# A scan and a two-layer network on one core: another plan of issue, other start

## The chip, the cores and the metric

The kernel runs on one core of a Trainium2 chip. Its time is the device time of the core in microseconds. TensorE (PE in the rows) does the matrix products, VectorE (DVE), ScalarE (ACT) and GpSimd (POOL) work on elements, and SyncE (SP) issues nearly all DMA transfers. Each engine takes its own instructions in the order in which they were issued; semaphores connect them.

## What is computed

Four batches of eight heads with 768 steps go through a scan with decay `a`, in chunks; its output, 3072 tokens of 256 values, goes through two matrices with `h - tanh(h)` between. The two matrices come in fp64 and are made into fp32 on the chip. Cut to what matters, with the reference's chunk length:

```python
log_a = np.log(np.clip(a, 1e-06, 1.0))
for c in range(nc):                      # chunks of the sequence
    cum = np.cumsum(la, axis=-1)
    L = np.exp(cum[:, :, :, None] - cum[:, :, None, :]) * causal
    M = np.einsum('bhin,bhjn->bhij', Cc, Bc) * L
    y[:, :, sl] = M @ xc + (Cc @ state) * np.exp(cum)[..., None]
    state = decay_full * state + sum_j(Bc_j x_j * decay_from_j)
h = x @ w_in                             # x: y as 3072 x 256; w_in: 256 x 2048
out = (h - np.tanh(h)) @ w_out           # w_out: 2048 x 256
```

## The kernel before

**Tiles.** The sequence is cut into chunks of 112 steps, and the 16 state rows of a chunk ride along as the first of 128 rows. There are 28 chunks (seven for each batch); the four batches' chunks follow one another, and their tokens make eight tiles, four of 256 and four of 512 tokens. Tiles 0 and 1, and 2 and 3, are worked as wide tiles 8 and 9 after the first sweep. The weights are cut into eight units of 256 columns of w_in and 256 rows of w_out. A sweep takes two units over tiles 0 to 3, so that the later units can be loaded and converted meanwhile; tiles 4 to 7 then run over all units.

**One chunk.** A mask `lt` (the exponential of differences of cumulated logs) is multiplied by the product `att` of B and C, cut to its causal part by GpSimd, and multiplied with x by TensorE into `y`. The product `z`, or eight more products behind `y`, gives the state that four small ScalarE copies put into the `x` of the chunk of the same batch that follows. For the first four chunks the mask comes from `fn_k`, `fn_f` and `fn_x` in `first_tile` (lines 445 to 471): GpSimd lays out the logs as `lm`, TensorE multiplies them by a triangle into the bank `cp`, ScalarE takes exp. Chunks 4 to 9 get it by `chunk_a` from rows in `lt_c` and `rt_c`, later ones by a DMA and eight exps in `chunk_l`.

**Products with the weights.** fp32 values are split into a high part (`xh`, `wh`, `gh`) and a low part (`xl`, `wl`, `gl`), and a product is three products of parts (L767 for `x @ w_in`, called mm1; L848 for w_out, mm2). Units 0 and 1 with tile 0 (L760) and their w_out with tiles 0 to 3 (L838) are done in plain fp32 with unsplit `xf`, `wv` and `wf`. `conv` makes fp32 from the raw fp64 words: a scaled ScalarE copy `wv` (L326), a shift of the low word by 29 bits `wm`, by ScalarE for the units named in `EASED` (L332, an affine copy) and by VectorE for the others (L334), a clamp (L339), two joins of bits (L342, L349), and the split (L353, L356).

**Order.** `Order` collects every step with its engine, a cost in microseconds and the names it reads and writes. `schedule` plays the steps through by these costs, `search` does so 16 times with shaken priorities and keeps the shortest plan, and `issue` emits the steps in order of their planned starts. So costs and rules of the planner set the order on every engine. The hardware's waits come from the data, not from the plan.

Of the kernel before, what the change touches and what calls it, by code (L numbers as in the profile page):

```python
# [61 lines left out]
EASED = 0, 1, 2, 3  # L62


class Order:
# [3 lines left out]
    DMA_LATENCY, SEM, SEM_PE, RATE, FLIGHT = 0.8, 0.15, 0.28, 0.32e6, 8  # L69
    ROUNDS, JITTER, SEED, EARLY, LOOK = 16, 0.3, 39, 8.0, 0.5  # L70

    def __init__(self):
        self.ops, self.urge = [], []
        self.writer, self.readers, self.count, self.before = {}, {}, {}, {}
        self.fresh, self.taken, self.dead = {}, {}, set()
        self.whole, self.parts, self.made = {}, {}, {}
# [13 lines left out]
    def __call__(self, eng, cost, fn, r=(), w=(), dma=0, after=(), urge=0.0):  # L90
        i = len(self.ops)
        hard = {self.writer[n] for n in r if n in self.writer} | set(after)
# [24 lines left out]
        for n in (*r, *w):  # L117
            assert n not in self.dead and n not in self.fresh and n in self.writer, n
        for n in r:
            self.readers.setdefault(n, set()).add(i)  # L120
        deps = {j: self.lag(self.ops[j][0], eng) if j in hard else 0.0 for j in (hard | soft) - {i}}
        self.ops.append((eng, cost, fn, deps))
        self.urge.append(urge)
        if dma:
            self.urge.append(urge)

            self.ops.append(("DMA", max(0.25, dma / self.RATE), None, {i: 1.4, **{j: 0.0 for j in chain}}))
# [9 lines left out]
    def schedule(self, prio, back=False, hold=None):  # L137
# [9 lines left out]
        start = [0.0] * n  # L147
        free = {op[0]: 0.0 for op in self.ops}
# [7 lines left out]
        while done < n:  # L156
# [67 lines left out]
def tile_ssm_moe(ctx: ExitStack, tc: tile.TileContext, a, x, bn, bc, wts, out):  # L224
# [90 lines left out]
    def conv(u, halves=False):  # L315
# [43 lines left out]
        for i in range(n):  # L359
# [3 lines left out]
            op("ACT", 1.0 * k, lambda s=s: fn0(s), r=n_r, w=[n_v[i]])  # L363
            op(*(("ACT", 1.02 * k) if u in EASED else ("DVE", 0.7 * k)), lambda s=s: fn1(s), r=n_r, w=[n_m[i]])
            op("DVE", 0.65 * k, lambda s=s: fn2(s), w=[n_v[i]])
            op("DVE", 1.2 * k, lambda s=s: fn3(s), r=[n_v[i]], w=[n_m[i]])
            if whole(s):
                op("DVE", 1.2 * k, lambda s=s: fn4(s), r=[n_m[i], n_v[i]], w=[f"wf{u}"])
                continue
            op("DVE", 1.2 * k, lambda s=s: fn4(s), r=[n_m[i]], w=[n_v[i]])  # L370
            op("ACT", 1.05 * k, lambda s=s: hi(s), r=[n_v[i]], w=n_h)
            op("DVE", 1.2 * k, lambda s=s: lo(s), r=[n_v[i]] + n_h, w=n_l)


    def parted(u, after):
# [63 lines left out]
    def first_tile():  # L439
# [38 lines left out]
        for ck in range(FIRST):  # L478
# [19 lines left out]
    def chunk_a(ck):  # L498
# [40 lines left out]
    def chunk_l(ck):  # L539
# [21 lines left out]
        if ck < NCK - NB:  # L561
            op("POOL", 0.6, fn_b, r=["wdec", "bi", d["n_b"]], w=n_l)
        op("ACT", 2.2, fn_e, r=["ncum", "tab"], w=n_l)
        op("POOL", 1.1, lambda: cut(ck), w=n_l)

    def state(G):
# [17 lines left out]
        op("PE", 0.55, fn, r=[*d["p_x"], d["n_bw"]], w=[n_z])  # L584
        for i in range(4):
            op("ACT", 0.22, lambda i=i: fn_c(i), r=[n_z], w=grp[G + NB // CPG]["p_x"])
# [31 lines left out]
    def split_x(after=()):  # L618
# [4 lines left out]
        op("DVE", 0.2 + 0.0018 * w, lambda: nc.vector.tensor_tensor(out=xl[:, :, 0:w], in0=xf[:, :, 0:w],  # L623
# [3 lines left out]
    def chunk_y(ck):  # L627
# [29 lines left out]
        cost = 0.48 if apart else 0.68  # L657
        if ck == JOINT - 1:
            n_a = slot("att", 1)
            op("PE", cost + 0.92, lambda: (cross(JOINT), fn()), r=r + [grp[JOINT // CPG]["n_bc"]], w=w + [n_a])  # L660
# [32 lines left out]
    def pair_y(ck):  # L693
# [28 lines left out]
        if ck + CPG < NCK:  # L722
            n_a = slot("att", 1)
            op("PE", 1.85, lambda: (cross(ck + CPG), fn()), r=r + [grp[G + 1]["n_bc"]], w=w + [n_a])
# [20 lines left out]
    def mm1(t, f):  # L745
# [7 lines left out]
        def fn():  # L753
            ph = ps_h.tile([P, BANK], F32, tag="ph", name=f"ph{t}_{f}")
            gs[t, f] = [ph]
            for i in range(blocks(t)):
                u, j = divmod(f + i, 2)
                if plain(t, f):
                    for k in range(2):
                        nc.tensor.matmul(out=ph[:, i * w : i * w + w], lhsT=part(slice(0, 1), wv[u]).rearrange(  # L760
# [443 lines left out]
```

## Time and profile before

| what | us |
|---|---|
| median of three runs | 321.63 (321.43 to 322.7) |
| the profiled execution, its own time | 322.48 |
| span of that execution | 320.8 |
| TensorE busy | 313.2 |
| ScalarE busy | 213.5 |
| VectorE busy | 210.7 |
| GpSimd busy | 59.2 |

[...] In a timeline row the first number is the start after the beginning of the span, the second how long the row lasts; behind the engine stand the line, the operation, what is written from what, and the count. TensorE counts an fp32 product as two records, and a record's length holds its latency, so what a product costs is read from one start to the next. A bracket at the end tells the engine's idle time before the row and what ended it.

### The profile page before, as it was taken

The numbers are of one execution on the slowest core, as the hardware profiler recorded it, in microseconds if no ns is written. First come the engines' busy times: TensorE is split into PE (matmuls) and PEld (weight loads), VectorE is DVE, ScalarE is ACT, GpSimd is POOL, SyncE is SP. The second block draws the span as 40 slices with busy tenths as digits, with TensorE's granted clock in tenths as the row PEclk, the third lists the DMA queues.
The fourth block names the chain that finished last, engine by engine and source line by source line (L and its number), as shares of the span: only waits on it lengthen the run. The fifth ranks groups of instructions, "written<-read, shape, count | busy, mean of one in ns | idle before, by whom it ended". The sixth has DMA issues, their size and how long they took to land.

```text
span 320.8 us, 5761 instructions
## 1 busy us (share of the span) xinstructions
PE 313.2 (98%) x2160; PEld 255.3 (80%) x2160; DVE 210.7 (66%) x308; ACT 213.5 (67%) x477; POOL 59.2 (18%) x94
## 2 busy tenths in 40 slices
PE   8889999999999999999999999999999999999995
PEld 7767887888888878787878878878878788888883
DVE  6978883998898856566654864664756645645551
ACT  5778989577698888578746854956868544544451
POOL 8533323002223424412101300201102000000000
PEclk9999999999999999999999999999999999999999
DMA  6869474649623347470606005007410000100001
GB/s 213 271 219 307 132 216 137 210 153 352 136 51 65 54 125 208 80 211 33 206 0 210 1 2 208 1 2 244 174 39 0 2 0 1 67 0 0 0 2 65
DMA packets 15452, 35.27 MB, mean 110 GB/s; under 512 B 2465, under 2 KB 4417, under 8 KB 15425
## 3 DMA queue, kind: packets, MB, share of 16 engines
q1 hardware_dynamic: 13696, 31.76, 29.7%
q0 software_dynamic: 1728, 3.15, 5.7%
q8 instruction: 17, 0.28, 0.3%
q14 instruction: 11, 0.08, 0.1%
HBM read 28.32 MB, written 3.43 MB: 99 GB/s over the span
## 4 chain that ended last, share of the span: by engine, by line
PE 94%; DVE 2%; DMA 2%; ACT 1%; issue 0%; SPq 0%; DVEq 0%
PE ph L767 41%; PE o L848 38%; PE o L838 5%; PE y L708 3%; PE att L682 3%; DMA raw<-w_d 2%; PE cp L455 1%; PE ph L760 1%; PE y L641 1%; DVE lt L475 1%; PE att L516 1%; PE att L465 1%; PE cp L452 0%; PE att L511 0%; DVE wv L349 0%
## 5 line engine op out<-in xcount | busy, mean ns | idle before, releaser
L802 DVE TENSOR_TENSOR g<-ph,g 128x512 f32<-128x512 f32 x96 | 65.8, 689 | 52.3 <-ACT g L798 52.0
L798 ACT ACTIVATE g<-ph 128x512 f32<-128x512 f32 x96 | 57.2, 596 | 51.8 <-PE ph L767 51.6
L812 DVE TENSOR_TENSOR gl<-g,gh 128x512 fp32r<-128x512 f32 x88 | 62.2, 710 | 29.7 <-ACT gh L806 28.8
L767 PE MATMUL ph<-xh,wh 128*128 128x512 f32 (+1 forms) x200 | 76.0, 383 | 0.0
L767 PE MATMUL ph<-xh,wl 128*128 128x512 f32 (+1 forms) x200 | 74.8, 377 | 0.0
L806 ACT CAST gh<-g 128x512 fp32r<-128x512 f32 x88 | 54.3, 619 | 27.3 <-DVE g L802 25.2
L848 PE MATMUL o<-gh,wh 128*128 128x512 f32 x176 | 69.2, 393 | 0.0
L848 PE MATMUL o<-gl,wh 128*128 128x512 f32 x176 | 68.5, 389 | 0.0
L848 PE MATMUL o<-gh,wl 128*128 128x512 f32 x176 | 68.5, 389 | 0.0
L767 PE MATMUL ph<-xl,wh 128*128 128x512 f32 (+1 forms) x200 | 59.1, 377 | 0.0
L536 POOL TENSOR_SCALAR_AFFINE_SELECT lt<-lt 128x896 f32<-128x896 f32 (+1 forms) x24 | 23.7, 989 | 130.5 <-ACT lt L554 119.9
L767 PEld LDWEIGHTS ph<-xh,wh 128*128 128x128 f32 x200 | 37.6, 188 | 7.5 <-issue 0.6
L767 PEld LDWEIGHTS ph<-xh,wl 128*128 128x128 f32 x200 | 37.6, 188 | 6.8
L767 PEld LDWEIGHTS ph<-xl,wh 128*128 128x128 f32 x200 | 36.8, 188 | 7.2 <-DVE xl L612 0.2
L554 ACT ACTIVATE lt<-lt,ncum 128x112 f32<-128x112 f32 (+1 forms) x144 | 41.7, 374 | 0.0
L848 PEld LDWEIGHTS o<-gh,wh 128*128 128x128 f32 x176 | 33.0, 188 | 7.7 <-issue 0.8
L848 PEld LDWEIGHTS o<-gl,wh 128*128 128x128 f32 x176 | 33.0, 188 | 7.0
L848 PEld LDWEIGHTS o<-gh,wl 128*128 128x128 f32 x176 | 33.1, 188 | 6.7
L688 DVE TENSOR_TENSOR lt<-att,lt 128x896 f32<-128x896 f32 (+1 forms) x18 | 18.9, 1052 | 5.1 <-POOL lt L536 5.1
L892 POOL DMA_DIRECT2D pt<-part x12 | 11.1, 1007 | 40.0 <-ACT part L889 39.8
L838 PE MATMUL o<-g,wf 128*128 128x256 f32 x64 | 15.5, 385 | 0.0
L609 ACT CAST xh<-y 128x224 fp32r<-128x224 f32 (+4 forms) x18 | 7.3, 411 | 11.0 <-DVE s L715 7.0
(98 smaller groups left out, 274.3 us busy)
## 6 DMA issues: line engine op xcount, KB each, us to landing
lt<-cumr SPq DMA_DIRECT2D x18, 512.0 KB
raw<-w_d SPq DMA_DIRECT2D x16, 512.0 KB
bc<-bc_d SPq DMA_DIRECT2D x14, 352.0 KB
x<-x_d SPq DMA_DIRECT2D x14, 256.0 KB
pt<-part POOLq DMA_DIRECT2D x12, 256.0 KB, 4.2
out_d<-ob SPq DMA_DIRECT2D x8, 256.0 KB
braw<-bn_d SPq DMA_DIRECT2D x14, 112.0 KB
out_d<-pt SPq DMA_DIRECT2D x4, 256.0 KB
```

The source lines that it names most:

```text
L536: nc.gpsimd.affine_select(out=k["l"][:, :, 0:q], in_=k["l"][:, :, 0:q], pattern=[[0, H], [1, q]], compare_op=ALU.is_ge, fill=0.0, base=N, ...
L554: nc.scalar.activation(k["l"][:, h, 0:q], k["l"][:, h, 0:q], AF.Exp, bias=ncum[:, h, ck : ck + 1])
L682: nc.tensor.matmul(out=a_[:, i], lhsT=bb[r], rhs=cc[r, :, 0 : qlen(ck)], start=True, stop=True)
L688: nc.vector.tensor_tensor(out=l, in0=chs[j]["a"], in1=l, op=ALU.mult)
L767: nc.tensor.matmul(out=ph[:, i * w : i * w + w], lhsT=w_[:, u, 0, k, j * P : (j + 1) * P], rhs=(xh, xl)[p][:, k, ts], start=p == 0 and k = ...
L798: nc.scalar.activation(g[:, 0:used], gs[t, f][0][:, 0:used], AF.Tanh)
L802: nc.vector.tensor_tensor(out=g, in0=ph, in1=g, op=ALU.subtract)
L806: nc.scalar.copy(gh[:, 0:used], gs[t, f][1][:, 0:used])
L812: nc.vector.tensor_tensor(out=gl[:, 0:used], in0=g[:, 0:used], in1=gh[:, 0:used].bitcast(F32), op=ALU.subtract)
L838: nc.tensor.matmul(out=po[t, seg][e], lhsT=wf[:, u, 256 * j + e * P : 256 * j + (e + 1) * P], rhs=gs[t, f][1][:, i * w : i * w + w], start ...
L848: nc.tensor.matmul(out=po[t, seg][e], lhsT=w_[:, u, 1, j, e * P : (e + 1) * P], rhs=g[:, i * w : i * w + w], start=f == seg[0] and k == 0 ...
L892: op("POOL", 1.0, lambda e=e: nc.gpsimd.dma_start(out=pts[m][:, e], in_=obs[t, e], accum_op=ALU.add), r=[name, n_pt[2 * m], n_pt[2 * m + 1 ...
```

## The change

It has five parts.

1. The planner's costs and rules. VectorE steps marked "DVE+" and GpSimd steps cannot run at once in the plan: the one that starts later is lengthened until the other is done. DMA transfers start sooner, run at 0.29 instead of 0.32 MB per us and end later when large. Many costs are set anew, and the seed is another. A step may also name inputs that it needs only towards its end (`late`, `by`).
2. mm1 takes all products with low parts of x last. For tiles of 256 tokens that moves the low parts of the first half behind the high parts of the second; for tiles of 512 tokens nothing moves. For the planner the low parts of x (and those of g in mm2) are late inputs.
3. `fn_k` and `fn_f`: the logs are laid out as 4 x 112 columns, and the triangle `after` is the weights of one product of 448 columns, where the logs were the weights of four products of 112 columns.
4. `EASED` is 1 and 2 instead of 0 to 3: the shift of units 0 and 3 goes from ScalarE to VectorE.
5. The three constant copies into `braw` are three steps with names of their own.

```diff
-EASED = 0, 1, 2, 3
+EASED = 1, 2
...
-    DMA_LATENCY, SEM, SEM_PE, RATE, FLIGHT = 0.8, 0.15, 0.28, 0.32e6, 8
-    ROUNDS, JITTER, SEED, EARLY, LOOK = 16, 0.3, 39, 8.0, 0.5
+    BIG, STRAGGLE, GRACE = 0.2e6, 0.5, 0.14
+    DMA_START, DMA_LATENCY, SEM, SEM_PE, RATE, FLIGHT = 0.65, 0.45, 0.15, 0.28, 0.29e6, 8
+    ROUNDS, JITTER, SEED, EARLY, LOOK = 16, 0.3, 81, 8.0, 0.5
...
+            if i in self.port and not back:
+
+                since, till = held["POOL" if e == "DVE" else "DVE"]
+                if since <= t < till - self.GRACE:
+                    free[e] = end = end + till - self.GRACE - t
+                held[e] = t, end
...
-            op("DVE", 1.2 * k, lambda s=s: fn3(s), r=[n_v[i]], w=[n_m[i]])
+            op("DVE+", 1.2 * k, lambda s=s: fn3(s), r=[n_v[i]], w=[n_m[i]])
...
-            chs[ck]["k", i] = p3.tile([P, BANK], F32, tag="g", name=f"lm{ck}_{i}").rearrange("p (h m) -> p h m", h=4)
-            nc.gpsimd.affine_select(out=chs[ck]["k", i], in_=la[:, 4 * i : 4 * i + 4, ck : ck + 1].broadcast_to([P, 4, P]),
-                                    pattern=[[0, 4], [-1, P]], compare_op=ALU.is_gt, fill=0.0, base=0, channel_multiplier=1)
+            lm = p3.tile([P, BANK], F32, tag="g", name=f"lm{ck}_{i}")
+            k = chs[ck]["k", i] = lm[:, 0 : 4 * Q].rearrange("p (h q) -> p h q", h=4)
+            nc.gpsimd.affine_select(out=k, in_=la[:, 4 * i : 4 * i + 4, ck : ck + 1].broadcast_to([P, 4, Q]),
+                                    pattern=[[0, 4], [1, Q]], compare_op=ALU.is_ge, fill=0.0, base=N, channel_multiplier=-1)
...
-            for h in range(4):
-                nc.tensor.matmul(out=f[:, h, 0:Q], lhsT=chs[ck]["k", i][:, h], rhs=upto[:, N:P], start=False, stop=h == 3,
-                                 skip_group_check=True)
+            nc.tensor.matmul(out=f[:, :, 0:Q], lhsT=after, rhs=chs[ck]["k", i], start=False, stop=True, skip_group_check=True)
...
-            for i in range(blocks(t)):
-                u, j = divmod(f + i, 2)
...
+            for p in range(1 if plain(t, f) else 2):
+                for i in range(blocks(t)):
+                    u, j = divmod(f + i, 2)
                     for k in range(2):
...
                         for w_ in (wh, wl)[: 2 - p]:
                             nc.tensor.matmul(out=ph[:, i * w : i * w + w], lhsT=w_[:, u, 0, k, j * P : (j + 1) * P],
-                                             rhs=(xh, xl)[p][:, k, ts], start=p == 0 and k == 0 and w_ is wh,
-                                             stop=p == 1 and k == 1, skip_group_check=True)
+                                             rhs=(xh, xl)[p][:, k, ts], start=p == i == k == 0 and w_ is wh,
+                                             stop=p == k == 1 and i == blocks(t) - 1, skip_group_check=True)
...
-    def stay():
-
-        for t in braws:
-            nc.gpsimd.tensor_copy(out=t[0:N].rearrange("p c (h n) -> p (c h) n", h=H),
-                                  in_=idn[0:N].unsqueeze(1).broadcast_to([N, CPG * H, N]))
+    def stay(t):
+
+        nc.gpsimd.tensor_copy(out=t[0:N].rearrange("p c (h n) -> p (c h) n", h=H),
+                              in_=idn[0:N].unsqueeze(1).broadcast_to([N, CPG * H, N]))
```

**The start.** SyncE's first transfers, before and then now; `raw0` are the fp64 words of weight unit 0, `bc0` the B and C of chunks 0 and 1, `cum3` the cumulated logs on their way out:

```order
L266 DMA bc0_136<-bc_d 128x704
L297 DMA raw0_138<-w_d 128x1024 x2
L278 DMA x0_155<-x_d 128x512
L266 DMA bc1_161<-bc_d 128x704
L266 DMA bc2_165<-bc_d 128x704
```

```order
L282 DMA bc0_150<-bc_d 128x704
L294 DMA x0_158<-x_d 128x512
L303 DMA braw0_106<-bn_d 112x256
L313 DMA raw0_170<-w_d 128x1024 x2
L1071 DMA cum3_115<-parts_111 112x3x128 x2
```

The weights moved behind x and B of the first chunks. ScalarE behind its second table load, before and then now; `lt0` is the mask of chunk 0, `cp0_0` and `cp0_1` the products of its two halves:

```order
L326 ACTIVATE wv0_188<-raw0_138 128x512
L332 ACTIVATE wm0_195<-raw0_138 128x512
L1080 ACTIVATE wdec_109<-pq2_179 128x224
L471 ACTIVATE lt0_206<-cp0_0_182 128x4x112
L326 ACTIVATE wv0_188<-raw0_138 128x512
```

```order
L1096 ACTIVATE wdec_109<-pq2_172 128x224
L486 ACTIVATE lt0_190<-cp0_0_175 128x4x112
L486 ACTIVATE lt0_190<-cp0_1_186 128x4x112
L486 ACTIVATE lt1_210<-cp1_0_192 128x4x112
L342 ACTIVATE wv0_217<-raw0_170 128x512
L486 ACTIVATE lt1_210<-cp1_1_214 128x4x112
L342 ACTIVATE wv0_217<-raw0_170 128x512
```

Three exponentials moved ahead of the first conversion, and the shift `wm0` left ScalarE.

**The first product of x @ w_in.** TensorE around `ph0_0`, tile 0 with unit 0, before (behind the last of four parts of chunk 4's mask product) and then now:

```order
L516 MATMUL att4_360<-bc2_165 128x224 x4
L641 MATMUL y2_374<-lt2_278,x1_232 32x112 x8
L576 MATMUL z0_388<-x0_155,bw0_284 16x32 x16
L760 MATMUL ph0_0_410<-xf_93,wv0_188 128x256 x4
L511 LDWEIGHTS lt_c_112
L511 MATMUL att5_423<-rt_c_113,lt_c_112 128x224
```

```order
L480 MATMUL att0_200<-bc1_212 128x224 x4
L656 MATMUL y1_300<-lt1_210,x0_158 32x112 x8
L656 MATMUL y2_310<-lt2_251,x1_220 32x112 x8
L776 MATMUL ph0_0_326<-xf_93,wv0_217 128x256 x4
L656 MATMUL y3_338<-lt3_280,x1_220 32x112 x8
L526 LDWEIGHTS lt_c_112
L526 MATMUL att4_351<-rt_c_113,lt_c_112 128x224
```

`ph0_0` moved ahead of y3, chunk 4's mask product and z0.

**Between the masks of chunks 4 and 5.** VectorE from `xl` of chunk 3 to the multiplication of chunk 5's mask, before and then now; `wv1` and `wm1` are unit 1, `g0_0` and `g0_2` tile 0 after tanh:

```order
L612 TENSOR_TENSOR xl_92<-y3_350,xh_91 128x2x112
L524 TENSOR_TENSOR lt4_384<-att4_360,lt4_384 128x8x112
L339 TENSOR_SCALAR wv1_307<-wv1_307 128x512
L342 SCALAR_TENSOR_TENSOR wm1_317<-wv1_307,wm1_317 128x512
L802 TENSOR_TENSOR g0_0_432<-ph0_0_410,g0_0_432 128x512
L524 TENSOR_TENSOR lt5_455<-att5_423,lt5_455 128x8x112
```

```order
L627 TENSOR_TENSOR xl_92<-y3_338,xh_91 128x2x112
L817 TENSOR_TENSOR g0_0_348<-ph0_0_326,g0_0_348 128x512
L539 TENSOR_TENSOR lt4_364<-att4_351,lt4_364 128x8x112
L355 TENSOR_SCALAR wv1_290<-wv1_290 128x512
L358 SCALAR_TENSOR_TENSOR wm1_334<-wv1_290,wm1_334 128x512
L365 SCALAR_TENSOR_TENSOR wf_94<-wv1_290,wm1_334 128x512
L817 TENSOR_TENSOR g0_2_399<-ph0_2_367,g0_2_399 128x512
L539 TENSOR_TENSOR lt5_419<-att5_401,lt5_419 128x8x112
```

The second join and `g0_2` moved ahead of chunk 5's multiplication, and `g0_0` ahead of chunk 4's.

## Rows read from the trace of the kernel before

**Rows 1.** The page: busy time of the engines, the chain that ended last by engine, and the groups of tanh and of the subtraction (busy us, mean ns of one).

```profile
PE 313.2 (98%) x2160; PEld 255.3 (80%) x2160; DVE 210.7 (66%) x308; ACT 213.5 (67%) x477; POOL 59.2 (18%) x94
...
PE 94%; DVE 2%; DMA 2%; ACT 1%; issue 0%; SPq 0%; DVEq 0%
...
L802 DVE TENSOR_TENSOR g<-ph,g 128x512 f32<-128x512 f32 x96 | 65.8, 689 | 52.3 <-ACT g L798 52.0
L798 ACT ACTIVATE g<-ph 128x512 f32<-128x512 f32 x96 | 57.2, 596 | 51.8 <-PE ph L767 51.6
```

**Rows 2.** Busy time by stretch: the stretch, its length, then PE, PEld, DVE, ACT and POOL busy, the granted clock, the DMA share and GB/s.

```profile
4.00:8.00 4.00, 4.00 (x33) 3.43 (x32) 3.47 (x6) 1.86 (x3) 3.72 (x7) 1.00 0.92 307
...
64.00:80.00 16.00, 16.00 (x72) 13.25 (x71) 14.83 (x21) 11.31 (x19) 2.37 (x3) 1.00 0.73 252
...
110.00:320.00 210.00, 206.96 (x1210) 167.96 (x1208) 119.96 (x177) 128.39 (x296) 23.36 (x34) 1.00 0.24 74
```

**Rows 3.** TensorE's waits over the whole span: who waited for whom, us in total, times, longest.

```profile
PE cp L452 <- ACT lt L471: 1.0, 1, 1.0
PE z L576 <- DVE xl L612: 0.9, 1, 0.9
...
PE att L682 <- PE ph L767: 0.7, 1, 0.7
```

**Rows 4.** TensorE's timeline from the sums of the logs to the mask product of chunk 6.

```profile
4.90 0.55 PE L1041 MATMUL pr<-la,upto 128*128 128x224 f32 x2
5.28 0.54 PE L1041 MATMUL pq<-la,after 128*128 128x224 f32 x2
5.66 0.35 PE L452 MATMUL cp<-never,eye 128*128 128x448 bf16 x1
5.85 1.04 PE L455 MATMUL cp<-upto,lm 128*128 128x112 f32 x8
6.72 0.35 PE L452 MATMUL cp<-never,eye 128*128 128x448 bf16 x1
...
22.25 1.99 PE L760 MATMUL ph<-xf,wv 128*128 128x256 f32 x8
...
27.62 0.28 PE L511 MATMUL att<-rt_c,lt_c 9*128 9x224 bf16 x4
```

**Rows 5.** TensorE's timeline from tile 1 to the end of tiles 0 to 3 in the first sweep.

```profile
33.42 0.38 PE L767 MATMUL ph<-xh,wh 128*128 128x256 f32 x1
...
36.48 0.28 PE L511 MATMUL att<-rt_c,lt_c 9*128 9x224 bf16 x4
...
37.09 0.59 PE L641 MATMUL y<-lt,x 128*32 128x112 f32 x16
37.49 0.30 PE L648 MATMUL y<-x,bw 128*16 128x32 f32 x16
...
51.49 0.47 PE L767 MATMUL ph<-xh,wh 128*128 128x256 f32 x1
...
55.64 1.04 PE L682 MATMUL att<-bc 32*128 32x224 f32 x16 [0.67 <-PE ph L767]
...
63.76 0.58 PE L767 MATMUL ph<-xh,wh 128*128 128x512 f32 x1
```

**Rows 6.** ScalarE's timeline at the start.

```profile
7.62 0.67 ACT L326 ACTIVATE wv<-raw 128x512 f32<-128x512 f32 x1 [2.13 <-DMA raw<-w_d]
8.19 0.66 ACT L332 ACTIVATE wm<-raw 128x512 uint32<-128x512 uint32 x1
...
8.99 0.54 ACT L471 ACTIVATE lt<-cp 128x448 f32<-128x448 f32 x1
...
22.40 1.06 ACT L582 COPY x<-z 16x128 f32<-16x128 f32 x4 [0.63 <-PE z L576]
...
25.14 0.91 ACT L520 ACTIVATE lt<-att 128x896 f32<-128x896 f32 x1
```

**Rows 7.** The timelines of VectorE and, in the last row, of GpSimd.

```profile
13.46 1.14 DVE L475 TENSOR_TENSOR lt<-att,lt 128x448 f32<-128x448 f32 x2
...
24.66 0.69 DVE L342 SCALAR_TENSOR_TENSOR wm<-wv,wm 128x512 uint32<-128x512 uint32 x1
...
26.09 1.09 DVE L524 TENSOR_TENSOR lt<-att,lt 128x896 f32<-128x896 f32 x1
...
31.62 1.39 DVE L356 TENSOR_TENSOR wl<-wv,wh 128x512 fp32r<-128x512 f32 x1
...
59.78 0.69 DVE L334 TENSOR_SCALAR wm<-raw 128x1024 uint32<-128x1024 uint32 x1
...
31.48 0.98 POOL L536 TENSOR_SCALAR_AFFINE_SELECT lt<-lt 128x896 f32<-128x896 f32 x1 [0.56 <-DVE lt L524]
```

**Rows 8.** ScalarE's timeline in the first sweep: a conversion of a whole unit, and the exponentials of a late chunk.

```profile
39.08 1.14 ACT L326 ACTIVATE wv<-raw 128x1024 f32<-128x1024 f32 x1
...
51.02 2.34 ACT L554 ACTIVATE lt<-lt,ncum 128x112 f32<-128x112 f32 x8
```

**Rows 9.** SyncE's timeline: the issue of the two halves of the first weights.

```profile
2.19 0.91 SPq L297 DMA_DIRECT2D raw<-w_d  x2
```

**Rows 10.** The page's DMA issues: what is written from what, count, KB each.

```profile
x<-x_d SPq DMA_DIRECT2D x14, 256.0 KB
...
braw<-bn_d SPq DMA_DIRECT2D x14, 112.0 KB
```

More of the change, by code (lines that the diff above doesn't have):

```diff
@@ L75, in __init__ @@
         self.fresh, self.taken, self.dead = {}, {}, set()
-        self.whole, self.parts, self.made = {}, {}, {}
+        self.whole, self.parts, self.made, self.big = {}, {}, {}, {}
+        self.port = set()
     def slot(self, tag, bufs):
@@ L88, in pieces, with __call__ @@
         return self.parts[name]
-    def __call__(self, eng, cost, fn, r=(), w=(), dma=0, after=(), urge=0.0):
+    def __call__(self, eng, cost, fn, r=(), w=(), dma=0, after=(), urge=0.0, late=(), by=0.0):
         i = len(self.ops)
+        if eng in ("DVE+", "POOL"):
+            self.port.add(i)
+        eng = eng.rstrip("+-")
         hard = {self.writer[n] for n in r if n in self.writer} | set(after)
@@ L116, in __call__ @@
                 soft.add(self.made[whole])
-        for n in (*r, *w):
+        later = {self.writer[n] for n in late} - hard
+        hard |= later
+        for n in (*r, *late, *w):
             assert n not in self.dead and n not in self.fresh and n in self.writer, n
-        for n in r:
+        for n in (*r, *late):
             self.readers.setdefault(n, set()).add(i)
-        deps = {j: self.lag(self.ops[j][0], eng) if j in hard else 0.0 for j in (hard | soft) - {i}}
+        deps = {j: self.lag(self.ops[j][0], eng) + self.big.get(j, 0.0) - (min(by, self.ops[j][1]) if j in later else 0.0) if j in hard else 0.0 for j in (hard | soft) - {i}}
         self.ops.append((eng, cost, fn, deps))
@@ L125, in __call__ @@
             self.urge.append(urge)
[L127 removed]
+            self.ops.append(("DMA", max(0.25, dma / self.RATE), None, {i: self.DMA_START, **{j: 0.0 for j in chain}}))
+            if dma > self.BIG:
+                self.big[i + 1] = self.STRAGGLE
             for n in r:
@@ L656, in chunk_y @@
         r, w = [*k["n_l"], d["p_x"][cg], *([] if apart else [d["n_bw"]])], [n_y]
-        cost = 0.48 if apart else 0.68
+        cost = 0.45 if apart else 0.64
         if ck == JOINT - 1:
             n_a = slot("att", 1)
-            op("PE", cost + 0.92, lambda: (cross(JOINT), fn()), r=r + [grp[JOINT // CPG]["n_bc"]], w=w + [n_a])
+            op("PE", cost + 0.92, lambda: (cross(JOINT), fn()), r=[grp[JOINT // CPG]["n_bc"]], late=r, by=0.9, w=w + [n_a])
             crossed(n_a, JOINT)
@@ L775, in mm1 @@
             n = sorted({"xf" + k[2:] for k in n})
-            op("PE", 6.88 * 0.25 * blocks(t) / 2, fn, r=[*n, convs[f // 2]], w=[n_h])
+            op("PE", 7.7 * 0.25 * blocks(t) / 2, fn, r=[*n, convs[f // 2]], w=[n_h])
             return
-        op("PE", 12 * rate(w) * blocks(t), fn, r=[*n, f"wh{f // 2}.0", f"wl{f // 2}.0"], w=[n_h])
+        op("PE", (12 if 2 * w > BANK else 12.7) * rate(w) * blocks(t), fn, r=[*(k for k in n if k[1] == "h"), f"wh{f // 2}.0", f"wl{f // 2}.0"],
+           late=[k for k in n if k[1] == "l"], by=8 * rate(w) * blocks(t), w=[n_h])
     def native(t, f):
@@ L1072, in tile_ssm_moe @@
     op("DVE", 0.36, lambda: split(0), r=[n_pr], w=["rows"])
-    op("DVE", 1.4, lambda: [split(i) for i in range(1, 6) if i != 4], r=["rows"], w=["parts"])
+    op("DVE+", 2.2, lambda: [split(i) for i in range(1, 6) if i != 4], r=["rows"], w=["parts"])
     for i in range(2):
```

83 lines of the change are left out of this document (42 added, 41 removed).

## The prediction

> **What bounds the kernel now.** The engine shares come first: TensorE is busy for 313.2 us of a span of 320.8, and the chain that ended last runs over it for 94% [rows 1]. So the time can only fall where TensorE idles, or where its work gets shorter. The stretches show where it does not idle: from 64 us on it is busy without a gap, 16.00 of 16 us and then to about 316.96 (110 + 206.96) [rows 2]. VectorE is close behind in 64 to 80 us, with 14.83 of 16. What follows 64 us is therefore fixed work, the same in both plans, unless VectorE falls behind there; everything else is decided before. The waits of TensorE are few [rows 3]: 1.0 us of the first masks for ScalarE, 0.9 of z for VectorE, 0.7 of a later attention product. With the launch that is all that an order of issue can win, apart from shorter work.
>
> I compare at two landmarks. At 27.62 TensorE starts the mask product of chunk 6 [rows 4]; in both plans it has done the same blocks by then. At 63.76 [rows 5] it has done tiles 0 to 3 of the first sweep.
>
> **Start, shorter work.** A mask block took 1.06 us of TensorE (5.66 to 6.72), of which 0.19 is the bf16 product (5.66 to 5.85) [rows 4]. The change gives it one fp32 product of 448 columns with the triangle as weights. The trace has 224 columns in one piece: 4.90 to 5.28, 0.38. So 448 take 0.76, the block 0.95, and eight of them save 0.9 us, all on TensorE's path.
>
> Hidden edits at the start: GpSimd makes masks of 448 instead of 512 columns and puts off one of its three copies into braw, so the first mask is ready before 5 us, but TensorE comes to it only at 5.66 after the sums; were TensorE free, up to 0.5 us would come of it. The new costs of the planner touch nothing but the order.
>
> **Start, ScalarE.** Before, ScalarE stood at 7.62 for the first weights, converted them twice, and made the first mask exponential only at 8.99, though its product was done before 7 us [rows 4, 6]. Now the exponentials stand first, so the first comes near 6.8. The two shifts of unit 0 (0.66 us each [rows 6]) leave ScalarE and become VectorE shifts: 0.69 for 1024 columns [rows 7], so some 0.4 for each half.
>
> I walk the new order on TensorE with a mask product of 0.61 (36.48 to 37.09) and a y of 0.40 (37.09 to 37.49) [rows 5]. Mask blocks start at 5.66, 6.61 and 7.56; the product of chunk 0 at 8.5; the fourth block at 9.1 to 10.05. The product of chunk 1 waits for both multiplications of chunk 0 (9.2 + 1.14 [rows 7]): 10.5, a wait of 0.45. Two blocks, y0, a block, a product, a block lead to 15.8; chunk 2's multiplications end at 16.2, so again 0.4. A product, y1, y2 end at 17.8; ScalarE copies y2 to xf, some 0.5 with the handing over. The first product of x @ w_in then starts near 18.3, against 22.25 [rows 4]: four microseconds earlier.
>
> **Where that lead goes.** Before, the mask product of chunk 4 and y3 stood ahead of that product, now behind it. So chunk 4's mask starts near 20.6, and the second product of tile 0 runs to 23.2. ScalarE has exp of chunk 4 until 22.3, then two conversions (some 0.57 each in sequence, 0.67 alone [rows 6]), tanh 0.60 [rows 1] after 23.2, so 23.9, the four copies of z, 1.06, and exp of chunk 5, 0.91 [rows 6]: done at 25.8. z1 needs the bank of z0 and waits for the copies to 25.0, where TensorE was ready at 24.1: 0.9 us lost. VectorE multiplies chunk 4's mask until 23.4, then has the clamp (0.4), two joins (0.69 alone, some 0.6 in sequence [rows 7]), the subtraction of g (0.69 [rows 1]) and chunk 5's multiplication (1.09 [rows 7]). With nothing in the way that is bound by the exponential, 25.8 + 1.1, and the product of chunk 6 starts at 27.0. But GpSimd cuts chunk 4's mask from about 23.5, and in the trace a VectorE operation on SBUF beside such a cut took 1.39 instead of 0.69 [rows 7]: 0.70 more. Without any blocking 27.0, with the whole cut (0.98 [rows 7]) in front of the joins 27.9; I take the measured 0.70, hence 27.55. Against 27.62 that is 0.07 won, of the four microseconds. ScalarE and VectorE take them back.
>
> [...]
>
> **From chunk 6 to the end of the first sweep.** Before: 63.76 - 27.62 = 36.14. The work is the same, except:
> - Tile 3's 24 products took 51.49 to 55.64, 4.15 us, with a wait of 0.67 at the attention product behind them and a shorter one inside [rows 5]; 24 of them took 3.06 in tile 1 (33.42 to 36.48). Now a w_out block stands between them and the attention product, and the low parts come last, so 3.1: 1.05 won. Low parts last changes no count; what it wins is that wait. If a low part is still late, up to 0.2 comes back.
> - Two w_out blocks of tile 1 now stand together, and tile 2's no longer follow mm1. Neighbours of another kind cost 0.1 to 0.2: 0.25 lost in sum. One fewer return from fp32 to mm1 behind the landmark: 0.2 won.
> - Two new waits. In tile 2 ScalarE has exp, then the conversion of unit 3 (1.14 [rows 8]), then tanh; VectorE the multiplication, the moved shift (0.69) and then g. TensorE comes to its w_out block at 46.4, g at 46.7: 0.3. In tile 3 the row of eight exponentials (2.34 [rows 8]) stands ahead of tanh and g, so g is ready about 0.25 after TensorE. The bounds are nothing and 1.2 us for both, if the broadcast transfer of chunk 11 lands one microsecond later than its place.
>
> Sum: -1.05 + 0.25 - 0.2 + 0.55 = -0.45. With the 0.07 it is 0.52 us less. Later waits: the first w_out product of the wide tiles needs its low part near 64 and gets it about a microsecond early, so VectorE's shift of unit 3 there costs nothing; with that cover gone each microsecond would count in full.
>
> **Own time.** The profiled execution took 322.48 us, 1.68 around its span, and is 0.85 above the median of 321.63. The difference carries over: 322.0 for it, 321.1 for the median.
>
> **Rivals.**
> - The lead survives. If the engines behind TensorE are not late where I put them, chunk 6 starts at TensorE's own pace, 26.0 (my walk without the 0.9 already counted leaves 1.55), and the new waits of 0.55 vanish: 2.1 us less than my forecast: 319.0. For it: ScalarE starts its exponentials two microseconds earlier (8.99 before [rows 6]). Against: exp of chunk 5 came at 25.14 before [rows 6] and has the same work in front of it now.
> - Slower: the first weights come late. They were issued at 2.19 and used at 7.62 [rows 6, 9]. Now 256 + 112 KB go ahead of them [rows 10], at 307 GB/s [rows 2] 1.2 us, so 8.8. VectorE's shift on them now stands ahead of chunk 0's multiplications, which are ready at 9.2; from about 9.3 each microsecond of delay is one of the whole. If the first half lands with the second, 512 KB later (1.7 us), it is 10.5, the price 1.2 and the time 322.3. At 9.8 the gain is gone, from 11.4 the kernel is slower by half a per cent. Against: nothing else is queued behind them now.
> - The turns of VectorE and GpSimd change nothing, since no wait of TensorE hangs on them, and starting early and ending late cancel: 321.6.
>
> **How the numbers follow.** Forecast 0.57 (its own range 320.1 to 322.1), the lead survives 0.20, weights late 0.10, nothing 0.13. Half a per cent, 1.6 us, is what a measurement of this kernel can tell from no change. Below 320.0 lie the surviving lead and the lower edge of the forecast (0.27); above 323.2 the far end of late weights or of the transfer of chunk 11 (0.07); the rest, 0.66, is no change. The range 319.2 to 322.6 leaves out half of the surviving lead and the upper tail, some 0.18.
>
> **What would show it.** Right: cp blocks of 0.95; the first exponential near 6.9; the first product of x @ w_in near 18.3; TensorE waiting before z1 and before chunk 6's product, which starts at 27 to 28; no wait before the attention product of chunk 12; no gap after 64. Wrong, if chunk 6's product starts near 26 (then faster than half a per cent), if the multiplications of chunk 0 wait for a transfer, or if TensorE idles after 64 us for low parts.

## The result and the profile after

The changed kernel took 325.53 us in the median, the kernel before 321.62 beside it. Over the single executions the ratio is 1.0098, with a 95% interval from 1.0075 to 1.0121; the two medians alone give 1.012. So it is slower by 1%, where the forecast was 321.1 with a range from 319.2 to 322.6. One of its seven executions, the profiled one, took 1101 us, with TensorE busy for 1094.5 of them; it is left out, and the profile read here is that of the same kernel run again (`e1_after`: 325.27 us, span 323.5).

The page of the changed kernel, busy time of the engines as in [rows 1]:

```profile
PE 314.8 (97%) x2112; PEld 252.1 (78%) x2112; DVE 213.7 (66%) x311; ACT 212.4 (66%) x474; POOL 61.7 (19%) x94
```

TensorE has less work to do, since eight mask blocks are shorter, and yet it was busy for 1.6 us more. So its products took longer. Its busy time by stretch, with the columns of [rows 2], tells where:

```profile
24.00:28.00 4.00, 2.38 (x110) 1.67 (x109) 3.86 (x6) 3.76 (x10) 1.72 (x2) 1.00 0.35 82
28.00:32.00 4.00, 3.36 (x18) 2.59 (x18) 3.27 (x5) 2.71 (x9) 1.54 (x1) 0.67 0.72 225
32.00:36.00 4.00, 4.00 (x56) 3.00 (x54) 0.94 (x1) 1.09 (x4) 1.74 (x3) 0.90 0.55 213
...
64.00:80.00 16.00, 16.00 (x72) 13.27 (x72) 13.96 (x20) 10.81 (x18) 1.55 (x3) 1.00 0.51 167
80.00:110.00 30.00, 30.00 (x134) 24.86 (x133) 26.50 (x35) 23.90 (x48) 7.07 (x9) 1.00 0.57 146
110.00:320.00 210.00, 209.74 (x1222) 170.26 (x1221) 123.91 (x180) 130.76 (x303) 26.37 (x37) 1.00 0.23 70
```

The first of these stretches in the kernel before:

```profile
24.00:28.00 4.00, 4.00 (x98) 2.96 (x96) 3.43 (x5) 3.11 (x9) 0.75 (x1) 1.00 0.92 308
```

From 24 to 28 us TensorE now stands for 1.62 of 4 us, where it did not stand before. Behind that the granted clock, the third figure from the end, is 0.67 and 0.90: the only stretches below 1.00 while TensorE works. From 64 us on there is no gap in either kernel [rows 2], and TensorE ends at 319.74 (110 + 209.74) against 316.96: 2.78 us later, all of it from the first 64 us. In steps of 1 us (PE busy, clock, DMA share, GB/s):

```profile
27.00:28.00 1.00, 0.15 (x19) 1.00 0.46 74
28.00:29.00 1.00, 0.36 (x8) 1.00 0.57 203
29.00:30.00 1.00, 1.00 (x10) 0.70 0.51 92
30.00:31.00 1.00, 1.00 (x4) 0.50 0.79 221
31.00:32.00 1.00, 1.00 (x3) 0.50 1.00 384
32.00:33.00 1.00, 1.00 (x4) 0.60 1.05 407
33.00:34.00 1.00, 1.00 (x7) 1.00 0.99 393
```

Half speed, a granted clock of 0.50, comes behind the idling, between 29 and 30 us, and is over by 33; 1.7 us of TensorE's time go there (0.30 + 0.50 + 0.50 + 0.40 of the four microseconds). TensorE's waits, which answer to [rows 3]:

```profile
PE att L526 <- DVE lt L539: 1.5, 1, 1.5
PE warm L1022 <- PEq L1207: 0.8, 1, 0.8
PE z L591 <- POOL lt L551: 0.8, 1, 0.8
PE o L853 <- DVE g L817: 0.7, 2, 0.4
PE att L480 <- DVE lt L490: 0.6, 2, 0.3
PE ph L776 <- ACT xf L620: 0.5, 1, 0.5
```

And its timeline, which answers to [rows 4]:

```profile
4.37 1.20 PE L1052 MATMUL pr<-upto,la 128*112 128x128 f32 x4
5.36 0.62 PE L1057 MATMUL pr<-la,upto 128*128 128x224 f32 x2
...
6.19 0.35 PE L469 MATMUL cp<-never,eye 128*128 128x448 bf16 x1
...
7.13 0.35 PE L469 MATMUL cp<-never,eye 128*128 128x448 bf16 x1
...
8.07 0.35 PE L469 MATMUL cp<-never,eye 128*128 128x448 bf16 x1
...
9.11 0.66 PE L480 MATMUL att<-bc 32*128 32x224 f32 x8
...
19.30 1.99 PE L776 MATMUL ph<-xf,wv 128*128 128x256 f32 x8 [0.46 <-ACT xf L620]
...
26.08 0.43 PE L591 MATMUL z<-x,bw 128*16 128x32 f32 x32 [0.77 <-POOL lt L551]
...
28.64 0.28 PE L526 MATMUL att<-rt_c,lt_c 9*128 9x224 bf16 x4 [1.48 <-DVE lt L539]
...
29.34 5.41 PE L853 MATMUL o<-g,wf 128*128 128x256 f32 x16
34.68 0.59 PE L656 MATMUL y<-lt,x 128*32 128x112 f32 x16
```

The mask block is 0.94 (6.19 to 7.13) where it was 1.06. The first product of x @ w_in starts at 19.30, three microseconds earlier than before. z1 (line 591) and chunk 6's mask product (28.64) wait 0.77 and 1.48. Then comes the w_out pair of tile 0, sixteen records, most of their time at a granted 0.50: 5.34 us to the next start. In the kernel before the same pair took 3.96:

```profile
28.22 4.02 PE L838 MATMUL o<-g,wf 128*128 128x256 f32 x16
32.18 0.28 PE L511 MATMUL att<-rt_c,lt_c 9*128 9x224 bf16 x4
```

VectorE in the stretch of the two waits:

```profile
24.46 0.42 DVE L355 TENSOR_SCALAR wv<-wv 128x512 f32<-128x512 f32 x1
24.98 1.28 DVE L358 SCALAR_TENSOR_TENSOR wm<-wv,wm 128x512 uint32<-128x512 uint32 x1
26.29 0.69 DVE L365 SCALAR_TENSOR_TENSOR wf<-wv,wm 128x512 uint32<-128x512 uint32 x1
26.90 0.68 DVE L817 TENSOR_TENSOR g<-ph,g 128x512 f32<-128x512 f32 x1
27.50 1.08 DVE L539 TENSOR_TENSOR lt<-att,lt 128x896 f32<-128x896 f32 x1
```

ScalarE and GpSimd at the same time, the four copies of z0, the exponential of chunk 5 and the cut of chunk 4's mask:

```profile
24.94 1.04 ACT L597 COPY x<-z 16x128 f32<-16x128 f32 x4
26.00 0.92 ACT L535 ACTIVATE lt<-att 128x896 f32<-128x896 f32 x1
```

```profile
24.61 1.10 POOL L551 TENSOR_SCALAR_AFFINE_SELECT lt<-lt 128x896 f32<-128x896 f32 x1 [1.43 <-DVE lt L539]
```

VectorE has hardly a gap (it is busy for 3.86 of the 4 us from 24 to 28). The multiplication that chunk 6 waits for is the last of its rows, and the first join before it took 1.28 instead of 0.69 beside GpSimd's cut. The exponential that the multiplication needs is done at 26.92; the multiplication starts at 27.50.

The clock also varies between executions of this kernel. The eleven others of the result and of `e1_after`, by their mean clock: 0.997 to 1.000 with 323.75, 324.08, 324.10 us; 0.992 to 0.994 with 325.27 to 325.63 (six); 0.989 with 326.01 and 326.79. Of the 54 executions of the kernel before beside the experiments, 52 have 0.997 or more; the two others, with 0.995 and 0.994, are its two slowest, 323.58 and 324.25.

### The profile page after: what moved, and what is told of

Read it like the earlier page. It is cut to its first block, busy times and chain, and to the rows that moved or that the text cites. A ratio compares the mean times of both kernels' runs of the same rounds, so it can differ in the third digit from the quotient of the medians.

```text
span 1099.6 us, 5655 instructions
## 1 busy us (share of the span) xinstructions
PE 1094.5 (100%) x2112; PEld 577.4 (53%) x2112; DVE 214.2 (19%) x311; ACT 215.3 (20%) x474; POOL 59.5 (5%) x94
## 4 chain that ended last, share of the span: by engine, by line
PE 100%; DVE 0%; ACT 0%; issue 0%
PE ph L781 42%; PE o L863 39%; PE o L853 5%; PE y L723 3%; PE att L697 2%; PE cp L471 2%; PE y L656 1%; PE ph L776 1%; PE att L531 1%; PE warm L1022 1%; PE att L480 1%; PE cp L469 1%; PE y L663 0%; PE att L526 0%; PE pr L1052 0%; PE z L591 0%
## 5 line engine op out<-in xcount | busy, mean ns | idle before, releaser
L781 PE MATMUL ph<-xh,wl 128*128 128x512 f32 (+1 forms) x200 | 207.5, 1037 | 0.0
L781 PE MATMUL ph<-xh,wh 128*128 128x512 f32 (+1 forms) x200 | 206.7, 1033 | 0.0
L863 PE MATMUL o<-gh,wl 128*128 128x512 f32 x176 | 194.2, 1104 | 0.0
L863 PE MATMUL o<-gh,wh 128*128 128x512 f32 x176 | 193.3, 1098 | 0.0
L863 PE MATMUL o<-gl,wh 128*128 128x512 f32 x176 | 191.3, 1087 | 0.0
L781 PE MATMUL ph<-xl,wh 128*128 128x512 f32 (+1 forms) x200 | 180.3, 1040 | 0.0
L781 PEld LDWEIGHTS ph<-xh,wl 128*128 128x128 f32 x200 | 89.1, 445 | 69.3 <-issue 69.3
L781 PEld LDWEIGHTS ph<-xh,wh 128*128 128x128 f32 x200 | 87.7, 438 | 71.4 <-issue 70.6
L781 PEld LDWEIGHTS ph<-xl,wh 128*128 128x128 f32 x200 | 86.6, 452 | 67.7 <-issue 67.7
L863 PEld LDWEIGHTS o<-gh,wl 128*128 128x128 f32 x176 | 76.8, 436 | 67.3 <-issue 67.3
```

The source lines that it names most:

```text
L781: nc.tensor.matmul(out=ph[:, i * w : i * w + w], lhsT=w_[:, u, 0, k, j * P : (j + 1) * P], rhs=(xh, xl)[p][:, k, ts], start=p == i == k == ...
L863: nc.tensor.matmul(out=po[t, seg][e], lhsT=w_[:, u, 1, j, e * P : (e + 1) * P], rhs=g[:, i * w : i * w + w], start=f == seg[0] and k == 0 ...
```

## The experiments

Under "before" stands the median of the kernel before beside each run. The ratios go by the single executions and so differ a little from the quotients of the medians.

| run | median us | before | ratio, interval |
|---|---|---|---|
| e1_after | 325.35 | 322.08 | 1.0100 [1.0067, 1.0133] |
| e2_tri_before | 321.30 | 322.08 | 0.9980 [0.9958, 1.0002] |
| e3_oldtri_after | 326.14 | 322.08 | 1.0127 [1.0095, 1.0159] |
| e4_fill | 325.35 | 322.05 | 1.0098 [1.0074, 1.0122] |
| e5_oldmm1 | 325.77 | 322.05 | 1.0103 [1.0069, 1.0137] |
| e6_lt5first | 323.48 | 322.05 | 1.0050 [1.0030, 1.0069] |
| e7_oldplan | 321.36 | 322.05 | 0.9978 [0.9963, 0.9993] |
| e8_fill2 | 325.03 | 321.81 | 1.0111 [1.0094, 1.0128] |
| e9_noport | 325.64 | 321.81 | 1.0114 [1.0087, 1.0141] |
| e10_eased | 324.16 | 321.81 | 1.0085 [1.0055, 1.0115] |
| e11_seed39 | 325.82 | 321.81 | 1.0141 [1.0112, 1.0170] |
| e12_fill3 | 324.08 | 322.22 | 1.0054 [1.0032, 1.0076] |

**The order or the triangle.** Three runs: the changed kernel again, the kernel before with the new triangle alone (its order unchanged), and the changed kernel's order with the old triangle. The edit of `e2_tri_before` (the mask itself is laid out as in the change); `e3_oldtri_after` makes the reverse of it in the changed kernel:

```diff
-            for h in range(4):
-                nc.tensor.matmul(out=f[:, h, 0:Q], lhsT=chs[ck]["k", i][:, h], rhs=upto[:, N:P], start=False, stop=h == 3,
-                                 skip_group_check=True)
+            nc.tensor.matmul(out=f[:, :, 0:Q], lhsT=after, rhs=chs[ck]["k", i], start=False, stop=True, skip_group_check=True)
```

> The changed kernel once more, for a profile of an ordinary execution. Theory A (the clock): its order of work is worth about what I forecast, but TensorE is granted less than the full clock in a stretch of the first 30 us, because the new start leaves it idle between the mask products; then the profile shows a granted clock under 1.00 there, products of twice the length in it, and the loss of 2 to 4 us lies inside that stretch. Theory B (waits): the clock is 1.00 throughout, and TensorE waits 3 us or more longer than before between 8 and 60 us; then the product of chunk 6 starts after 29 us or a gap stands after 36 us.

> The kernel before with the triangle as weights alone: one product of 448 columns instead of four of 112 and masks of 448 columns, in exactly the old order. Theory A and theory B both say that the shorter product alone is no loss: TensorE's first 17 us hold the exponentials' pace, so the time stays within 0.5 us of before (321.1 to 322.1), the blocks become 0.95 us. If this alone lowers the granted clock, the time is 323 or more and the triangle is the cause.

> The changed kernel with the old mask product (logs as weights, four products of 112 columns) in exactly the new order. Theory A with the triangle as cause: the clock stays at 1.00 and the time falls to 322 or less. Theory A with the order as cause: the clock falls as in the changed kernel, and the time is 0 to 1 us above it, for eight blocks that are 0.1 us longer. Theory B: 0.3 to 0.9 us above the changed kernel, clock 1.00.

The triangle alone gives 0.8 us, close to the forecast's 0.9, though its interval just reaches 1. The new order loses with either triangle, and with the old one chunk 6 waits 1.57 and the clock falls again (0.75 and 0.82 in the two stretches from 28 to 36 us). So the loss is in the order.

**What the inner order of x @ w_in does.** The changed kernel with the old order inside the products, and the kernel before with both edits of single steps (triangle, low parts last) but none of the plan. The edit of `e7_oldplan` beside the triangle, taken back in `e5_oldmm1`:

```diff
-            for i in range(blocks(t)):
-                u, j = divmod(f + i, 2)
...
-                for p in range(2):
+            for p in range(1 if plain(t, f) else 2):
+                for i in range(blocks(t)):
+                    u, j = divmod(f + i, 2)
```

> The changed kernel with the products of x @ w_in in their old inner order (each half's low parts right behind its high parts), order of the steps unchanged. If taking the low parts last is neutral here: 325.0 to 325.8, waits in front of z1 and of chunk 6's product as before, clock falling at the same place. If it wins the wait inside tile 3's products, as in my forecast: 0.2 to 0.7 us slower, 325.6 to 326.1. If it loses something: faster by more than 0.4 us.

> The kernel before (its order, its costs) with the two changes to single steps only: triangle as weights, and low parts last inside the products of x @ w_in. If the loss lies in the order alone and both edits are small gains: clock 1.00 in all stretches from 20 to 40 us, the wait of 0.67 behind tile 3's products (and the one inside) is gone, and the time is 0.7 to 1.8 us below the kernel before, 319.8 to 321.0. If the low parts last are worth nothing: as the triangle alone, 321.0 to 321.5. Also asked of this profile: whether the first products at 4.37 us run at half speed (1.20 us, as in both profiles of the new order so far) or not (0.69, as in both of the old): by the order 0.69, by chance either.

Low parts last is worth nothing that can be measured: 325.77 without it, 325.35 with it, and 321.36 against 321.30 in the old order. There the wait behind tile 3's products is still 0.92 in `e7_oldplan`, so it was not the low parts that made it. In the traces of `e7_oldplan` and of the kernel before, the attention product behind them starts 0.10 after VectorE's last multiplication of a mask in front of it (ending at 54.50 and 55.54), which reads the one tile `att` that the product is about to overwrite. Both edits without the plan make the one version whose interval lies below 1, by 0.2%; the triangle alone has the same median within 0.1 us.

**Filling the idle stretch.** If the clock falls because TensorE stands, work put where it stands should bring the time down. Three runs put some there. In each the extra products write what is written anyway or is written over; no work is left out. `e4_fill` issues chunk 5's products of B and C twice and chunk 4's y five times:

```diff
-            for i in range(4):
+            for i in 2 * [0, 1, 2, 3] if ck == 5 else range(4):
...
-            for hg in range(2):
+            for hg in [0, 1] * (5 if ck == 4 else 1):
```

`e12_fill3` puts three wide products ahead of chunk 4's y, `e8_fill2` seven:

```diff
+            for _ in range(3 if ck == 4 else 0):
+                nc.tensor.matmul(out=y[:, 0:NHC], lhsT=after, rhs=laf, start=True, stop=True)
```

> The changed kernel with TensorE's idle stretch filled: chunk 5's products of B and C are issued twice and chunk 4's y products five times, each time with the same values into the same place, some 2 us more work where TensorE only waited (the waits in front of z1 and of chunk 6's mask product). Theory C (TensorE's clock falls because it idles for over 2 us of the 4 before 28.6 us, and that fall is most of the loss behind it): granted clock 1.00 in every stretch from 28 to 36 us instead of 0.67 and 0.90, the w_out pair of tile 0 lasts 3.9 to 4.1 us instead of 5.41, chunk 6's product starts where it did (28.4 to 29.0), and the time is 1.2 to 2.3 us below the changed kernel's 325.4, so 323.1 to 324.2. Theory W (the waits are the loss, the clock falls for another reason): clock still below 0.9 somewhere in 28 to 36 us, time 325.0 to 326.5.

> A better filling of the idle stretch. In the first one the fifth y products ran until 28.95 and then TensorE stood for another 1.43 us at nothing that the profile shows, which pushed chunk 6's product to 30.85. Here seven wide fp32 products (128x224, some 0.19 us each) are issued in front of chunk 4's y, into the place that y then overwrites: 1.3 us of work where TensorE waits 1.48. Theory C (clock): chunk 6's product stays at 28.5 to 29.0, granted clock 1.00 in 28 to 36, tile 0's w_out pair lasts 3.7 to 4.0, time 323.5 to 324.2, that is 1.2 to 1.9 below the changed kernel. Rival (the products only trade places: what is gained in the clock is lost in a later y or a new stall): clock 1.00, but time above 324.6.

> The seven products took 2.92 us, twice what I had reckoned (0.38 each), and pushed chunk 6's product to 29.57. Here it is three, 1.15 us where TensorE waits 1.48, so that nothing should be pushed. Clock theory: granted clock 1.00 in 28 to 36 us, chunk 6's product at 28.4 to 28.9 as in the changed kernel, tile 0's w_out pair 3.7 to 4.0 us instead of 5.41, executions at the time that the changed kernel had in its few executions with a clock of 0.999 to 1.000 (323.75, 324.08), so a median of 323.5 to 324.3, 1.1 to 1.8 below the changed kernel, and still about 2 us above the kernel before: that rest is the waits. If the clock is not what costs: 325.0 or more.

The first two kept the clock at 1.00, but were too long: they pushed chunk 6 to 30.85 and 29.57 and lost there what they won. Their times, 325.35 and 325.03, lie where their expectations put the rivals of the clock. The seven products took 2.84 us (26.09 to 28.93 on TensorE's timeline), not the 1.3 that were expected. The third fits. TensorE's timeline in `e12_fill3`:

```profile
25.58 0.43 PE L591 MATMUL z<-x,bw 128*16 128x32 f32 x32 [0.77 <-POOL lt L551]
25.94 1.40 PE L654 MATMUL y<-la,after 128*128 128x224 f32 x6
...
28.14 0.28 PE L526 MATMUL att<-rt_c,lt_c 9*128 9x224 bf16 x4 [0.16 <-DVE lt L539]
...
28.84 3.72 PE L855 MATMUL o<-g,wf 128*128 128x256 f32 x16
32.49 0.59 PE L658 MATMUL y<-lt,x 128*32 128x112 f32 x16
```

The pair takes 3.65 (28.84 to 32.49) instead of 5.34, though nothing that feeds it came sooner on account of the fill: the half microsecond by which chunk 6 is earlier was there at the first product of x @ w_in, 18.80 in this execution. All eight executions have a clock of 0.998 to 1.000, and the median of 324.08 is that of the changed kernel's three executions at full clock. The slowest, 324.43, is faster than the eight others of those eleven. Three useless products make the kernel 1.3 us faster: this shows the clock's share. About 1.9 us over the kernel before remain, and they are not the clock's.

**VectorE's queue.** In the changed kernel the multiplication of chunk 5's mask goes ahead of unit 1's second join and of g of columns 2.

```diff
# e6_lt5first
+        at = order.index(self.first)
...
+        order = [i for i in order[: at + 1] if i not in self.later] + self.later + order[at + 1 :]
```

> The changed kernel with three steps of VectorE exchanged: the multiplication of chunk 5's mask is issued ahead of unit 1's second join and of the subtraction for g of columns 2, so the wait in front of chunk 6's mask product loses what stood ahead of it. If the order of VectorE's queue is that wait: chunk 6's product starts 0.5 to 1.0 us earlier (27.6 to 28.1 instead of 28.64); the time falls by that, and by up to 1.4 more if the shorter idling keeps the clock up: 323.2 to 325.0. If w_out's first products then wait for the join instead, the wait only moves: chunk 6 earlier, but tile 0's w_out pair starts no earlier than 29.2 and the time is 325.0 to 326.0.

```profile
28.07 0.28 PE L535 MATMUL att<-rt_c,lt_c 9*128 9x224 bf16 x4 [0.95 <-DVE lt L548]
...
28.78 3.72 PE L866 MATMUL o<-g,wf 128*128 128x256 f32 x16
32.43 0.59 PE L667 MATMUL y<-lt,x 128*32 128x112 f32 x16
```

Chunk 6 started at 28.07, 0.57 earlier, with a wait of 0.95. That rest is ScalarE's: VectorE stood for 0.71 us until the exponential was done (26.90) before it multiplied. The profiled execution kept a clock of 1.00, as three of the other four did, the pair took 3.65, and the median is 323.48. So half a microsecond less of waiting won 1.9 us, which the wait alone can't give: with the clock up, the pair gives back the rest.

**Which part of the plan.** The changed kernel without the rule of turns, with the shift of all units on ScalarE, and with the planner's old random seed. Each makes another order. The three edits, in this order:

```diff
-            if i in self.port and not back:
+            if False and i in self.port and not back:
...
-EASED = 1, 2
+EASED = 0, 1, 2, 3
...
-    ROUNDS, JITTER, SEED, EARLY, LOOK = 16, 0.3, 81, 8.0, 0.5
+    ROUNDS, JITTER, SEED, EARLY, LOOK = 16, 0.3, 39, 8.0, 0.5
```

> The changed kernel with the rule of turns for VectorE and GpSimd taken out of the planner; its new costs, late inputs, triangle and EASED stay, so another order comes out (tile 0's first product stands behind chunk 4's mask product, its second behind chunk 6's). If the rule is what makes the start bad: the waits between 24 and 30 us shrink below 1.2 in sum, clock 1.00, 320.5 to 322. If the new costs or the late inputs are: still 2 us of waits somewhere before 40 us and a clock below 1, 323.5 to 326.

> The changed kernel with the shift of all four units on ScalarE as before (EASED 0 to 3), planner and the rest as changed; another order comes out of it. If moving unit 0's shift to VectorE makes VectorE late for chunk 5's mask (the wait of 1.5): that wait is below 0.7 and the time 321 to 323. If it is ScalarE and VectorE together that are short in 20 to 30 us, wherever the shift is: still 2 us of waits between 22 and 30, 323.5 to 326.

> The changed kernel with the planner's old random seed (39 instead of 81), all its rules and costs as changed: another order by the same rules. If the rules are sound and the plan of the change an unlucky one: 320.5 to 322.5, at least a microsecond under the changed kernel. If the rules lead to bad plans: 324 to 327, waits of over 2 us in sum before 40 us and a clock below 1 behind them.

All three are slower than the kernel before, and within what their expectations gave for another cause. In `e11_seed39` TensorE waits 0.77 and 1.00 ahead of chunk 6, and its windows (columns of [rows 2]) read:

```profile
24.00:28.00 4.00, 2.17 (x79) 1.43 (x78) 4.00 (x5) 2.76 (x5) 1.58 (x2) 0.96 0.92 325
28.00:32.00 4.00, 3.72 (x18) 2.71 (x18) 3.82 (x6) 3.73 (x11) 2.23 (x4) 0.50 0.84 262
32.00:36.00 4.00, 4.00 (x23) 2.90 (x21) 2.99 (x2) 0.57 (x2) 2.17 (x2) 0.69 0.00 1
```

`e9_noport` waits for other things (0.98 at a y for GpSimd's weights near 25, 1.1 at a w_out block); its ten executions run from 322.75 at a clock of 1.000 to 326.94 at 0.990. So neither the turns nor the seed nor the shift of units 0 and 3 is the cause by itself: four different plans by the new costs and late inputs wait between 23 and 29 us, and three of the four lose clock in most executions (the fourth, `e10_eased`, in one of four). Which of the many new costs does it was not tried.

## Why the prediction was wrong

**Right.** A mask block of 0.95 (0.94). Exponentials before the weights: the first at 7.33 instead of 8.99 (forecast 6.9; 6.53 in `e12_fill3`). Waits in front of z1 (0.9 forecast, 0.77) and of chunk 6's product (from 26.0 to 27.55 in the forecast, 1.48). z1 starts 0.10 behind ScalarE's copies of z0, as forecast; its row names the cut, which was over at 25.71. The join beside the cut was 0.59 longer (forecast 0.70, from [rows 7]). The join ended 0.55 after the cut (26.26 and 25.71), as the slowed operation of [rows 7] did in the kernel before (33.01 and 32.46). From the first product of x @ w_in to chunk 6 it is 9.34 us, for 9.25 in the forecast. New waits at w_out of tiles 2 and 3: 0.34 and 0.40 for 0.55 in sum. No wait ahead of chunk 12's attention product, and no gap after 64 us.

**The step that failed: a wait was priced at its length.** The forecast put 0.9 us of waiting before z1 and 1.55 before chunk 6, two and a half microseconds within four, and went on to "The work is the same, except". It never asked what TensorE's clock does behind such a stretch. In the profile of the kernel before it was 1.00 throughout, and no rival named it. The runs show in its place: half speed (0.50) between 29 and 33 us, behind the idling, which cost 1.69 us on the w_out pair (5.34 against 3.65 with the stretch filled) and 1.3 in the median. The idling was two short waits, 0.77 and 1.48 us, and in `e1_after` the products behind them still ran at a granted 1.00 for some 0.7 us (28.64 to about 29.4, an estimate from the mean of 0.70 between 29 and 30 us) before 0.50 was granted. How much waiting it takes was not shown.

**Terms that were too small.** With the clock at 1.00 the kernel is still 1.9 us slower than before, where the sum said 0.5 faster. In the profiles of `e12_fill3` and of the kernel before, TensorE ends 1.37 apart (318.33 and 316.96), so there the forecast missed by 1.9: 0.6 up to chunk 6 and 1.3 behind it.
- "The first product of x @ w_in then starts near 18.3": it was 19.30, and 18.80 in `e12_fill3`, whose first products ran fast. The walk took too little for the work. It counts a mask block as 0.95, a product as 0.61 and a y as 0.40, whatever stands behind. A block took 0.94 ahead of another block, but 1.04 ahead of a product of another kind (8.07 to 9.11). The eight blocks, four products and three y of the walk come to 11.24 us and took 12.05, without waits; the waits were right (1.38 in `e12_fill3` for some 1.35). Of these 0.8 us `e12_fill3` won 0.3 back with an earlier first block, at 5.38 for 5.66. The other 0.5 is passed on to chunk 6: 28.14 there for the forecast's 27.55.
- The first products themselves: 4.37 to 5.36 in this profile, 4.37 to 4.90 in [rows 4]'s execution, on the same instructions. It is no effect of the order: the row of the first sums (line 1052 here) lasts 0.66 to 0.70 in the profiles of before, e2, e5, e9, e11, e12, 1.19 or 1.20 in those of e1, e3, e4, e6, e7, and 0.87 to 0.89 in e8 and e10. A landmark taken from one execution carries 0.5 us of such chance.
- "1.05 won" at tile 3: the wait behind the products went, because a w_out block now stands there, but in `e12_fill3` one of 0.78 stands ahead of them. The forecast had it only as a bound, a late broadcast transfer ahead of ScalarE's row of exponentials, and at the w_out blocks. From chunk 6 to TensorE's end `e12_fill3` takes 0.85 longer than the kernel before (290.19 for 289.34), where the sum has 0.45 won. Of these 1.3 us 0.78 is this wait, and 0.2 the longer waits at w_out. The w_out blocks of tiles 0 to 3 account for most of the rest: without waits they take 14.64 us instead of 14.25, where the sum has 0.05 for their neighbours.

TensorE and ScalarE of `e12_fill3` there:

```profile
53.32 0.39 PE L783 MATMUL ph<-xh,wh 128*128 128x256 f32 x1 [0.78 <-ACT xh L624]
```

```profile
49.70 2.34 ACT L569 ACTIVATE lt<-lt,ncum 128x112 f32<-128x112 f32 x8 [0.71 <-DMA lt<-cumr]
52.06 0.85 ACT L671 COPY x<-y 16x64 f32<-16x64 f32 x4
52.92 0.34 ACT L624 CAST xh<-y 128x224 fp32r<-128x224 f32 x1
```

The chain reads from the transfer through the exponentials and the copies to xh. That the transfer is its cause was read from the rows and not tried. In `e1_after` the same place has no wait, because TensorE arrives two microseconds later: the lost clock hides the second stall. So of the pair's 1.69 us some 0.8 comes back as this wait. TensorE's ends in the two profiles are still 1.41 apart (319.74 and 318.33), since 0.5 of that is the faster start of `e12_fill3`; how the 1.3 of the medians divides is not shown.

What stays open: the waits of `e12_fill3` to 64 us are 2.3 longer than in the kernel before (0.94 by the windows, and 1.33 that the fill covers), its work some 0.9 shorter, most of it in the mask blocks. That accounts for the 1.37 at the end, but not for why the new plan has 2.3 us more of waits. The forecast had seen their places but for the one at tile 3, and their lengths to some 0.2.

**Of the rivals**, "the turns change nothing" and "the lead survives" fell: the order moved much, and the three microseconds won at 19.30 were gone by 28.64. "The first weights come late" did not happen: ScalarE took them at 9.65 without a wait. The slower side was right in sign only, by a mechanism that was not on the list.

## What to carry to other kernels

A plan that starts the bound engine earlier than its suppliers can follow may turn one long lead into several stalls, here 0.77 and 1.48 us; where such stalls stand close together, price TensorE's clock behind them too, by what the next block costs at half speed, here 5.34 us for 3.65. A stall can be worth more than its length: half a microsecond less of waiting gave 1.9 here. Take a block's price where the same kind of work stands behind it, here 0.94 or 1.04. Look at the granted clock of single executions before comparing medians: it sorted the times of this kernel into three groups by itself.

## What was not expected

- A few products without any use made the kernel faster by 1.3 us (`e12_fill3`): with them the granted clock was 0.998 to 1.000 in all eight executions, without them 0.989 to 0.994 in eight of eleven.
- In `e4_fill` TensorE stood for 1.43 us in the middle of a chunk's small products, and the profile shows nothing that it waited for. TensorE's timeline there:

```profile
28.95 0.28 PE L663 MATMUL y<-x,bw 128*16 128x32 f32 x11
...
30.67 0.24 PE L663 MATMUL y<-x,bw 128*16 128x32 f32 x5 [1.43 <-issue]
```

It came behind forty y products in a row (80 records). Why was not settled.
- The first products, between 4.1 and 4.5 us, take 0.66 or 1.20 us, which changes from profile to profile. The granted clock reads 1.00 there in all of them, so that the clock makes the difference is not shown.
